# Two column groups in the last stage of a long convolution, identity products at the start, and a new order of work

## The chip, the core and the metric

The kernel runs on one core of one Trainium2 chip. The time is the device time of the slowest core in microseconds (us), here of the only one. TensorE (PE in the profile; PEld is its weight load), VectorE (DVE), ScalarE (ACT), GpSimd (POOL) and SyncE (SP) each work through a queue of their own, in order; 16 DMA engines move data for the transfers that SP and POOL issue.

## The reference, cut to what matters

Two independent heads share the kernel, each of 2048 positions and 1024 channels; their outputs stand side by side.

```python
def _A_ref(q, k, v, shift_k, ssm_k, ssm_D):
    ...
    for t in range(ks):
        k_shift = k_shift + k_pad[:, t:t + S, :] * shift_k[:, ks - 1 - t][None, None, :]
    kv = k_shift * v
    ...
    y_f = kv_f * kf_f[None, :, :, :]
    ...
    y = y + kv * ssm_D[None, None, :]
    return q * y

def _B_ref(x, Lambda_re, Lambda_im, B_re, B_im, C_re, C_im, log_dt, Dskip):
    ...
    for t in range(L):
        h = Lam_bar[None, :] * h + Bu[:, t, :]
    ...
    y = 2.0 * jnp.einsum("blp,dp->bld", hseq, Cmat).real + x * Dskip[None, None, :]
    return y
```

In A, kv_f and kf_f are Fourier transforms along the sequence, padded to 4096; y is the inverse transform of their product. In B, h is a complex state of 1024 entries, and Lam_bar and Bu come from the parameters.

## The kernel before, in words

All work is cut into words such as `U.9.3.0` or `a3.6.0`. The string ORDER (line 67) lists 1504 words; the loop at the end of full_kernel calls the function of each word's name with its numbers (E["a3"](6, 0)). The words' order in the string is thus, engine by engine, the order of each queue: TensorE's, VectorE's, ScalarE's, and also SP's and POOL's, which issue the DMAs. Behind a colon stand the buffers that a word takes: `p3` is PSUM bank 3 (of 8; 128 partitions by 512 columns of 32 bits), `a28` is unit 28 of an arena in SBUF (53 units of 128 by 1024 bf16), `h` and `w` are slots for B's state chunks and for transform weights. A word waits where its data or its buffer is not free. No word is moved at run time.

**Head A** is a transform in stages. kp and vp load k and v; kvm, kva, kvb, kvc (VectorE) make kv for one of 16 residues n2 of the position. Its first three need the shift weights on all partitions: ld_w loads them into one row, wb (TensorE, products with a row of ones, 512 columns) spreads them, wbe (ScalarE) copies them out. Stage 1: am (TensorE, four products of 512 columns in two words for each n2), ae (ScalarE evicts a bank), ast (POOL stores to the DRAM tile Ys_kv). The filter goes the same way, with hl, hT, hc, hm, he, hst, into Ys_h. Stage 2 works on 32 groups, two to a load, 16 loads: lh and lk (SP) read Ys_h and Ys_kv, sh and sk (TensorE, line 650) are transforms of 64 by 64 in the four quadrants of the array, eight products of 512 columns each; she and ske evict; sw (POOL) swaps rows by DMA; pr (VectorE, line 677) multiplies; sa (TensorE, line 689, eight quadrant products) and sae go back; vst (POOL) stores to Vs. No lk can start before all ast have landed, and no vl before all vst.

The last stage: vl (SP, line 705) loads 512 KB of Vs for one of 16 n2; a3 (line 717) makes 512 output columns for all 128 positions of this residue, by two products that add up in one bank. Each takes a weight Gt[:, p, :] of 128 columns, of which those of the other parity are zero. a3e (line 724, ScalarE) evicts; qm or qh (VectorE) multiplies with q, which qp loaded; osp or oh (SP, lines 734 and 732) stores.

**Head B** works in 16 chunks of 128 positions. bl loads the matrix B in 16 parts, bT transposes a part on TensorE by eight products with the identity (line 397), bc copies it out; cl, cT, cc and cx do so for C. Parameters come by ld_par (four small DMAs on SP), par_T (one product, line 255), p32 (VectorE, line 260) and small words; tabA1, tabA2 and sm_pre are tables on VectorE. x (SP) loads a chunk transposed; xs and xl put some chunks aside in DRAM. U (line 444) multiplies it with B: a word is half of a bank, 16 products of 128 columns; ue evicts. r1, r2, sc, r3, r4 (VectorE) rotate, scan along time and rotate back; cy carries the last state over. y (line 527 and, for the skip term, 530) multiplies with C: a word is four products of 512 columns and one of 128, eight words a chunk. For chunks 6 to 12 the word is yt (lines 498 and 512) instead: 16 quadrant products, and 16 small ones in the last part. ye evicts, yst, ysp or yh store 512 or 256 KB.

Of the kernel before, what the change touches and what calls it, by code (L numbers as in the profile page):

```python
# [71 lines left out]
bc.3.0 bl.1.1:a44 bT.1.1:p3 sin1 kva.2 kvb.2:a34 bl.7.1:a46 bT.7.1:p4 bc.3.1 bl.4.0:a45 bT.4.0:p6 bl.7.0:a1 U.0.1.1 bc.1.1 U.0.0.1 bc.7.1 bT.7.0:p7
bc.4.1 bc.4.0 kvb.1:a1 sin2 x.5:a32 U.5.0.0:a50p3 U.5.0.1 U.5.1.0:p4 U.5.1.1 U.5.3.0:p6 bc.7.0 U.5.3.1 U.0.3.1 bl.5.1:a33 bT.5.1:p1 eo ue.5.1 vp.1:a48
bc.5.1 kp.-2 kvm.0:a44 kvc.2 ue.0.3 cl.0.1:a10 kvc.3 cl.1.1:a11 cT.1.1:p7 x.1:a0 U.1.0.0:a48p4 bl.5.0:a9 cx.5.1 kva.0 ue.5.0 bT.5.0:p1 bc.5.0 U.1.0.1
ue.1.0 cT.0.1:p2 cc.0.1 ue.5.3 U.1.2.0:p1 U.1.2.1 cc.1.1 U.1.3.0:p4 U.5.2.0:p6 U.0.2.0:p2 U.0.2.1 stt z2 U.5.2.1 z1 ue.0.1 x.2:a37 ue.0.0 kp.2
kvm.5:a28 kvm.4:a8 vp.0:a38 kvc.1 U.2.0.0:a42p3 U.2.2.0:p7 kvb.0:a36 U.2.3.0:p5 U.2.3.1 U.1.1.0:p0 cl.1.0:a40 kva.4 ue.0.2 r1.0:a4 ue.1.2 ue.5.2 kva.5
gz U.1.1.1 r2.0:h0 dd U.2.1.0:p2 ue.2.3 cx.4.0 am.1.0:p6p5 kvb.5:a41 cx.6.1 rt U.1.3.1 cl.0.0:a33 cT.0.0:p1 sc.0.1 U.2.1.1 ae.1.1.0:a2 ue.1.1 cc.0.0
cl.3.0:a16 cT.3.0:p5 ue.1.3 U.2.2.1 sc.0.0 r1.1:a28 ue.2.1 am.3.1:p4p1 cx.7.0 cc.3.0 ae.1.0.0 r3.0:a16 r2.1:h1 am.1.1:p2p0 ae.1.1.1 r4.0 U.2.0.1
ue.2.0 kvc.0 cT.1.0:p5 cl.2.0:a44 cT.2.0:p6 cc.1.0 x.3:a45 U.3.0.0:a46p0 U.3.2.0:p3 cc.2.0 cl.2.1:a5 cT.2.1:p5 U.3.0.1 cc.2.1 cl.3.1:a4 cT.3.1:p6
ae.3.0.1:a48 ue.2.2 U.3.2.1 ae.1.0.1 am.2.0:p4p5 cc.3.1 U.3.1.0:p2 cx.6.0 U.3.3.0:p7 y.0.0.0:p6 y.0.0.1 r1.2:a16 U.3.3.1 cx.7.1 cy.1 ae.2.0.0:a6  # L80
sc.1.1 sc.1.0 ae.2.1.0 am.2.1:p4p5 ue.3.3 ae.2.0.1 ue.3.0 y.0.0.2 y.0.0.3 kvb.4:a44 am.0.0:p4p7 r3.1:a28 ue.3.2 ae.0.0.0:a4 ae.0.1.0 U.3.1.1 cx.5.0
cx.4.1 y.0.1.0:p0 ue.3.1 vp.2:a38 y.0.1.1 y.0.1.2 kp.3 ae.2.1.1 y.0.1.3 am.3.0:p3p4 kvc.5 am.0.1:p7p2 r4.1 ae.0.0.1 ae.3.1.0 y.1.0.0:p5 ae.0.1.1
ae.3.1.1 kvc.4 y.1.1.0:p7 am.4.0:p4p2 y.1.0.1 y.1.1.1 r2.2:h2 y.1.1.2 hl.1:a42 y.1.1.3 r1.3:a8 ye.0.0:a40 y.1.0.2 cy.2 ae.3.0.0 sc.2.1 am.4.1:p1p3
# [715 lines left out]
```

## Time and profile before

| | us |
|---|---|
| median of 3 runs | 347.86 |
| runs | 347.36 to 350.82 |
| profiled execution, whole | 351.36 |
| its span, first to last instruction | 349.6 |
| TensorE busy in the span | 334.9 |
| VectorE busy in the span | 314.1 |

A line of the profile names the engine, the line of the kernel, the operation, what it writes and reads, and how often; behind a bar stand the group's busy time in us and the mean length of one in ns, then the idle time of the engine before it and what ended that. One product's length holds its way through the pipeline; how fast products follow each other is read from the chain of waits or the timeline, where neighbours are merged into one row (start, length, count). "Granted clock" is the share of TensorE's full clock that the record shows.

### The profile page before, as it was taken

What the parts mean: (1) busy time and instruction counts of PE and PEld (TensorE: products, weight loads), DVE (VectorE), ACT (ScalarE), POOL (GpSimd) and SP (SyncE); (2) the same over time, 40 slices, a digit from 0 to 9 for tenths busy, and PEclk for the clock granted to TensorE, in tenths of its full rate; (3) what the DMA queues carried; (4) which work ended last, traced back from release to release, by engine and by line L of the source; (5) the groups of instructions that cost most, each with busy time, mean ns of one, the idle gap of its engine ahead of it and who ended that gap; (6) DMA issues with size and microseconds to landing.
All of it is one profiled execution on the core that took longest, in us unless ns stands there. A gap on an engine that the chain in (4) does not pass through costs nothing. (4 is left out here: it accounts for less than half of the span.)

```text
span 349.6 us, 10684 instructions
## 1 busy us (share of the span) xinstructions
PE 334.9 (96%) x4540; PEld 236.7 (68%) x4561; DVE 314.1 (90%) x240; ACT 285.2 (82%) x547; POOL 79.4 (23%) x130
## 2 busy tenths in 40 slices
PE   5899999999999999999987999999999999999996
PEld 3799998546765767748863565786668676865442
DVE  4899999999999999999996997979985968997992
ACT  6999997468698999987884889999998887537672
POOL 5000000032334337055231004223233151300100
PEclk9999999999999999999998999999999999999999
DMA  6999967599999999999869599989989999779977
GB/s 204 336 297 257 239 157 79 225 263 281 289 317 295 370 273 316 314 259 303 301 229 367 181 335 310 364 304 347 384 322 321 368 400 344 281 264 389 344 299 266
DMA packets 63691, 103.07 MB, mean 295 GB/s; under 512 B 29550, under 2 KB 31870, under 8 KB 63644
## 3 DMA queue, kind: packets, MB, share of 16 engines
q1 hardware_dynamic: 52348, 63.98, 61.6%
q0 software_dynamic: 11296, 38.42, 30.0%
q8 instruction: 35, 0.57, 0.7%
q14 instruction: 12, 0.10, 0.1%
HBM read 53.09 MB, written 34.60 MB: 251 GB/s over the span
## 5 line engine op out<-in xcount | busy, mean ns | idle before, releaser
L444 PEld LDWEIGHTS <-BT 128*128 128x128 bf16 x2048 | 117.5, 98 | 11.3 <-issue 4.5
L444 PE MATMUL bank<-arena,BT 128*128 128x128 bf16 x2048 | 123.2, 219 | 1.2 <-ACT arena L446 0.5
L472 DVE TENSOR_TENSOR_SCAN gslot<-rtab,gslot 128x1040 bf16<-128x1040 f32 x32 | 73.0, 2310 | 3.0 <-ACT gslot L468 2.8
L527 PE MATMUL bank<-CT,gslot 128*128 128x512 bf16 x279 | 68.4, 379 | 0.7 <-DVE gslot L478 0.2
L498 PE MATMUL bank<-CT,gslot 64*64 64x512 bf16 x896 | 57.4, 384 | 0.0
L446 ACT CAST arena<-bank 128x512 bf16<-128x512 f32 x64 | 40.0, 659 | 13.3 <-PE bank L444 13.2
L677 DVE TENSOR_TENSOR arena<-arena 128x4096 bf16<-128x4096 bf16 x16 | 36.2, 2285 | 10.8 <-ACT arena L667 7.7
L527 PEld LDWEIGHTS <-gslot 128*128 128x128 bf16 x288 | 26.0, 98 | 27.8 <-DVE gslot L478 0.9
L667 ACT CAST arena<-bank 128x512 bf16<-128x512 f32 x64 | 38.5, 685 | 6.6 <-PE bank L650 6.6
L498 PEld LDWEIGHTS <-gslot 64*64 64x64 bf16 x896 | 29.8, 109 | 19.2 <-issue 1.7
L589 ACT CAST arena<-bank 128x512 bf16<-128x512 f32 x64 | 35.7, 632 | 7.8 <-PE bank L583 6.0
L459 DVE TENSOR_TENSOR arena<-arena,Z 128x4096 bf16<-128x4096 bf16 x16 | 36.5, 2282 | 4.7 <-ACT arena L446 4.2
L660 ACT CAST arena<-bank 128x512 bf16<-128x512 f32 x64 | 37.7, 731 | 3.5 <-PE bank L650 3.4
L627 ACT CAST arena<-bank 128x512 bf16<-128x512 f32 x64 | 36.2, 632 | 4.8 <-PE bank L621 4.7
L697 ACT CAST arena<-bank 128x512 bf16<-128x512 f32 x64 | 38.7, 738 | 0.9 <-PE bank L689 0.9
L459 DVE TENSOR_TENSOR arena<-gslot,Z 128x4096 bf16<-128x4096 bf16 x16 | 36.6, 2289 | 1.0
L671 POOL DMA_DIRECT2D arena<-arena x32 | 17.4, 546 | 79.5 <-ACT arena L660 75.3
L563 DVE TENSOR_TENSOR arena<-arena 128x4096 bf16<-128x4096 bf16 (+3 forms) x16 | 30.0, 1885 | 1.2 <-DMA arena<-in_A_k_dram 0.7
L592 POOL DMA_DIRECT2D Ys_kv<-arena x16 | 11.4, 719 | 86.2 <-ACT arena L589 86.2
L630 POOL DMA_DIRECT2D Ys_h<-arena x32 | 23.2, 737 | 24.9 <-ACT arena L627 24.9
L650 PE MATMUL bank<-arena,wslot 64*64 64x512 bf16 x256 | 24.3, 388 | 3.6 <-DMA arena<-Ys_kv 3.2
L536 ACT CAST arena<-bank 128x512 bf16<-128x512 f32 x32 | 20.1, 651 | 8.4 <-PE bank L530 4.7
(101 smaller groups left out, 414.6 us busy)
## 6 DMA issues: line engine op xcount, KB each, us to landing
Ys_kv<-arena POOLq DMA_DIRECT2D x16, 512.0 KB, 5.6
Ys_h<-arena POOLq DMA_DIRECT2D x32, 256.0 KB, 4.7
arena<-Ys_h SPq DMA_DIRECT2D x16, 512.0 KB, 5.5
arena<-arena POOLq DMA_DIRECT2D x32, 256.0 KB, 4.8
...
```

Of the source, the lines that this page charges most:

```text
L444: nc.tensor.matmul(pu[:, w, jl, :], BT[:, 2 * jp + jl, w, d, :], xT[:, d, :], start=(d == 0), stop=(d == ND - 1))
L446: E["ue"] = lambda i, jp: nc.scalar.copy(st["u", i][:, :, 2 * jp:2 * jp + 2, :], st.pop(("pu", i, jp)))
L459: nc.vector.tensor_mul(m, s_, win(Z))
L472: nc.vector.tensor_tensor_scan(gf, rtab[:].rearrange("p j t -> p (j t)"), gf, 0.0, ALU.mult, ALU.add)
L498: mm = nc.tensor.matmul(st["py", i, dh][64 * c:64 * c + 64, :], h[rows, w, j, 2 + 64 * c:66 + 64 * c], CT[rows, j, w, dh * 512:(dh + 1) * ...
L527: nc.tensor.matmul(py, h[:, w, j, 2:GW], CT[:, j, w, dh * 512:(dh + 1) * 512], start=(j == 0 and w == 0), stop=False)
L589: return nc.scalar.copy(st["ysb", n2][:, p, dh * 512:(dh + 1) * 512], st.pop(("pa", n2, p, dh)))
L627: return nc.scalar.copy(st["yh", hf, s][:, p, e, :], st.pop(("pb", hf, s, e, p)))
L660: return nc.scalar.copy(st["hab", i][:, 0, a, l, :], st.pop(("ps", "h", g, l)))
L667: return nc.scalar.copy(st["x16", i][:, a, l, :], st.pop(("ps", "k", g, l)))
L677: nc.vector.tensor_mul(hab, st.pop(("x16", i)).rearrange("p a l d -> p (a l d)").unsqueeze(1).to_broadcast([P, 2, 2 * D]), hab)
L697: return nc.scalar.copy(st["vsb", i][:, a, dh * 512:(dh + 1) * 512], st.pop(("pv", g, dh)))
```

## The change

Four things are done together.

1. G holds for each parity p only the 64 weight columns of its own positions. a3 writes the product with parity p to partitions 64 p to 64 p + 63 of the bank, as a product of its own: 128 rows and 64 columns of the array, without adding up. The 128 partitions then hold the even positions, then the odd ones.
2. qp, oh, osp (and ost, which no word uses) move these rows by two DMAs, one for each parity, of half the bytes each: 17 DMAs more in all.
3. A word wu.n is new: n products of the identity with itself, 128 columns, into a bank that the next word overwrites. Eight of them hold 66 products, all ahead of the first U.
4. ORDER is written anew, 1512 words; words other than wu are the same (beside the tasks that yf names, behind which a yt word is fenced). The tile praw lies in a weight slot.

In the new order ld_par stands behind bl.0.0 and par_T behind five wb words; x.0 stands behind nine bl and three kp words (before: nine and two). The last kv product of VectorE is kvc.12, behind sc.6.0 (before: kvc.14, ahead of sc.6). From the last am word to the first sk, TensorE's words are six U, six sh and six yt (before: seven U, six sh, four yt). yst.7, yst.9, yst.10 and yst.11 stand behind the last vst (before: yst.9; yst.12 and yst.13 do in both), qp.0 among the a3 words (before: all qp ahead of the first vl). Behind the last sa stand 6 yt, 12 U, 24 y and 32 a3 words (before: 2, 10, 24, 32); the a3 words stand in four runs with y and U words between.

```diff
@@ a_constants
-    G = np.stack([tr.T * (m % 2 == p)[None, :] * 2 / NFFT for p in range(2)], axis=1)
+    G = np.stack([tr.T[:, m % 2 == p] * 2 / NFFT for p in range(2)], axis=1)
@@ full_kernel
-    Gt = const.tile([P, 2, P], BF16, name="Gt")
+    Gt = const.tile([P, 2, P // 2], BF16, name="Gt")
...
-        praw = const.tile([4 * NJ, P], BF16, name="praw")
+        praw = wslots[1][0:4 * NJ, 0:P]
...
+    def wu(n):
+        pt = bank()
+        for _ in range(n):
+            nc.tensor.matmul(pt[:, 0:P], ident[:], ident[:], start=True, stop=True)
+    E["wu"] = wu
...
-        spd(st["qt", r], qr[:, 2 * r:2 * r + 2, :])
+        for p in range(2):
+            spd(st["qt", r][64 * p:64 * p + 64, :, :], qr[p::2, 2 * r:2 * r + 2, :])
...
-            nc.tensor.matmul(pt, Gt[:, p, :], st["vv", n2][:, p, dh * 512:(dh + 1) * 512], start=(p == 0), stop=(p == 1))
+            nc.tensor.matmul(pt[64 * p:64 * p + 64, :], Gt[:, p, :], st["vv", n2][:, p, dh * 512:(dh + 1) * 512], start=True, stop=True)
...
-    E["oh"] = lambda n2: spd(oar[:, n2, :], st["ot", n2 // 2][:, n2 % 2, :])
-    E["ost"] = lambda r: gpd(oar[:, 2 * r:2 * r + 2, :], st["ot", r])
-    E["osp"] = lambda r: spd(oar[:, 2 * r:2 * r + 2, :], st["ot", r])
+
+    def halves(dma, rows, tile):
+        for p in range(2):
+            dma(rows[p::2], tile[64 * p:64 * p + 64])
+    E["oh"] = lambda n2: halves(spd, oar[:, n2, :], st["ot", n2 // 2][:, n2 % 2, :])
+    E["ost"] = lambda r: halves(gpd, oar[:, 2 * r:2 * r + 2, :], st["ot", r])
+    E["osp"] = lambda r: halves(spd, oar[:, 2 * r:2 * r + 2, :], st["ot", r])
@@ ORDER
-ld_w:a8 ld_par wb.0:p1 wbc:a12 wb.4:p5 par_T:p2 p32 ld_F wbe.0 wb.7:p3 wb.2:p4 wbe.4 exp1 dve2 dve3 wbe.2 wbe.7 tabA1:a16a18a4a6 sm_pre wb.3:p0
-wb.5:p7 wbe.5 exp2 wbe.3 bl.6.0:a52 bT.6.0:p2 wb.6:p6 kring:a20 bc.6.0 bl.1.0:a1 bl.0.0:a0 bT.0.0:p1 bc.0.0 bl.0.1:a3 bT.0.1:p5 bc.0.1 wbe.6 bl.2.1:a2
-bl.3.0:a52 bT.3.0:p7 kva.3 x.0:a35 kp.-1 kvm.2:a40 kvm.1:a28 bT.2.0:p1 U.0.0.0:a2p0 U.0.3.0:p2 bc.2.0 U.0.1.0:p5 kvb.3:a52 bl.4.1:a0 kva.1 bT.4.1:p1
...
-U.9.0.1 ae.13.0.1 U.7.2.0:p6 ae.13.1.1 U.7.2.1 x.15:a10 hst.1.2.0 am.12.0:p3p2 ae.13.0.0 ae.15.0.0 kva.14 U.7.1.1 r1.6:a12 kvb.14:a0 r2.6:h0 kvc.14
-hst.1.2.1 ue.7.1 hst.1.3.1 am.12.1:p7p0 U.9.1.0:p5 U.9.1.1 ae.14.1.1 ae.14.0.0 ae.14.1.0 U.9.2.1 ue.7.3 ae.12.1.1 hst.1.4.1 hst.1.3.0 sc.6.0 yst.4
-r3.6:a24 ae.12.0.1 hst.1.7.0 ue.9.2 hst.1.4.0 hst.1.5.1 hst.1.5.0 ast.13 lh.1:a28 sh.2:p0p1 sh.3:p3p4 she.2.1:a12 she.2.0 she.3.0 she.3.1 lh.0:a18
-she.1.1 sh.7:p5p3 U.10.0.0:a4p0 U.10.0.1 r2.7:h1 cy.7 she.6.1:a20 ast.15 ast.14 she.7.1 she.7.0 ast.12 sw.1.0 she.6.0 ue.9.3 lk.1:a44 sk.3:p2p7
...
-sw.12.0 sw.14.1 pr.14 sa.28:p5p3 sae.28.1:a48 sae.28.0 sa.29:p6p1 sae.29.1 sae.29.0 sw.12.1 yf.yt.12.ue.13.2 yt.12.1.0 pr.12 sw.13.0 sa.25:p4p7
-sw.13.1 yst.6 pr.13 sa.27:p3p5 yst.7 yt.12.1.1 yst.11 sa.26:p6p1 sae.25.1:a6 sae.27.1:a18 sa.24:p7p5 yt.12.1.2 yt.12.1.3 sae.27.0 U.15.0.0:a44p3
-U.15.0.1 sae.26.1 U.15.2.0:p1 sae.26.0 U.15.2.1 U.14.1.0:p6 r1.13:a32 U.14.1.1 r2.13:h2 cy.13 sae.25.0 U.15.1.0:p4 U.15.1.1 sae.24.1 sae.24.0 sc.13.1
...
-r1.14:a32 r2.14:h0 cy.14 sc.14.1 ye.12.0:a46 ue.15.1 ue.15.2 sc.14.0 ye.12.1 qp.7:a8 r3.14:a24 qp.2:a30 vst.14 vst.13 vst.12 r4.14 yst.9 vl.6:a18
-a3.6.0:p3 a3.6.1:p4 a3e.6.0:a20 a3e.6.1 vl.10:a10 a3.10.0:p2 a3e.10.0:a18 ye.13.0:a17 vl.12:a4 a3.12.1:p1 a3.10.1:p6 a3.12.0:p3 a3e.12.1:a10 vl.14:a14
...
-osp.0 osp.6 a3e.7.0 qm.3 y.15.0.2 osp.3 a3e.11.1 a3e.11.0 qm.5 a3e.9.1 y.15.0.3 qm.4 ye.15.0:a52 osp.4 osp.5 yh.15.0 y.15.1.1 a3e.15.0 y.15.1.2
-a3e.15.1 y.15.1.3 qh.15 ye.15.1 oh.15 yh.15.1
+ld_w:a8 wbc:a12 wu.18:p4 wb.2:p4 wu.2:p3 wb.4:p3 wbe.2 bl.0.0:a52 wu.2:p0 wb.7:p0 wbe.7 wu.2:p7 wb.3:p7 wu.2:p6 wb.0:p6 wbe.4 ld_F ld_par par_T:p1 p32
+exp1 bT.0.0:p4 wbe.3 dve2 dve3 tabA1:a18a16a4a6 sm_pre bl.6.0:a1 bT.6.0:p3 bc.6.0 bl.6.1:a3 bl.0.1:a2 bl.4.0:a0 wu.2:p5 wb.5:p5 bT.0.1:p1 bc.0.1 tabA2
+bT.6.1:p0 bc.6.1 wb.1:p7 bl.1.1:a28 wb.6:p3 bT.1.1:p2 kring:a20 wbe.1 bl.1.0:a29 wbe.5 kp.0 kp.1 wbe.6 bl.2.1:a52 bc.1.1 wbe.0 exp2 kvm.3:a36
+bT.1.0:p1 bl.4.1:a1 bc.0.0 bc.1.0 kp.-1 kvm.1:a44 kva.3 wu.31:p0 bT.4.1:p0 kvm.2:a40 kva.1 bT.2.1:p2 kvb.3:a1 kva.2 sin0 bc.2.1 bT.4.0:p1 par_rest
+x.0:a31 kvb.2:a30 sin1 kvb.1:a52 gz wu.7:p7 U.0.0.0:a28p7 U.0.3.0:p3 bl.2.0:a3 bT.2.0:p5 bc.2.0 U.0.0.1 bl.7.1:a2 bT.7.1:p4 sin2 bl.3.1:a32 bT.3.1:p2
...
+U.7.1.0:p1 ue.7.0 sc.6.0 am.15.1:p3p6 U.7.1.1 ae.13.1.0:a42 ae.13.0.0 am.15.0:p4p0 ae.13.1.1 lw.3:w1 ae.15.1.1:a8 kvc.12 ae.13.0.1 ae.15.0.1 hst.1.1.0
+U.7.3.0:p2 U.7.3.1 yst.4 sc.6.1 U.7.2.0:p6 ae.15.0.0 am.14.1:p7p3 U.7.2.1 ae.15.1.0 r3.6:a12 hst.1.7.1 am.14.0:p4p0 ue.7.3 hst.1.1.1 ue.7.1 x.10:a11
+ae.14.1.1:a46 hst.1.2.1 ue.7.2 U.9.0.0:a32p3 lw.2:w3 U.9.3.0:p1 am.12.1:p2p6 ae.14.0.0 ae.14.1.0 am.12.0:p4p0 ae.14.0.1 ae.12.0.1:a34 U.9.1.0:p7
+ae.12.0.0 x.15:a10 U.9.2.0:p2 ae.12.1.0 U.9.1.1 lw.0:w2 U.9.2.1 ae.12.1.1 U.9.0.1 hst.1.2.0 hst.1.3.0 hst.1.3.1 hst.1.4.0 hst.1.5.1 hst.1.7.0 ye.5.1
+hst.1.4.1 ue.9.1 hst.1.5.0 ue.9.2 ast.13 ast.15 lh.1:a2 sh.3:p6p4 sh.2:p5p7 she.2.0:a24 she.3.1 ue.9.0 r4.6 yt.6.0.0:p0p2 yt.6.0.1 yt.6.0.2 she.3.0
+she.2.1 r1.7:a20 r2.7:h1 lh.0:a30 sh.0:p3p4 cy.7 sh.1:p5p7 lh.3:a28 yt.6.0.3 she.1.0:a4 sh.7:p5p6 she.1.1 ast.14 ast.12 she.0.1 U.9.3.1 she.0.0
+she.7.0:a12 sh.6:p7p3 she.6.1 yf.yt.6.she.7.0 yt.6.1.0 yt.6.1.1 xs.15 lk.1:a2 she.7.1 she.6.0 sk.2:p6p3 ske.2.1:a8 lk.0:a46 sk.3:p7p4 ske.3.0 yt.6.1.2
...
+yt.12.0.1 sw.13.0 sw.13.1 pr.13 sae.24.1:a30 sa.27:p3p1 sae.24.0 sae.25.1 sa.26:p7p6 sae.25.0 yt.12.0.2 yt.12.0.3 U.15.0.0:a8p0 U.15.0.1 U.15.3.0:p2
+U.15.3.1 sae.27.1:a36 r1.13:a20 U.14.3.0:p1 U.14.3.1 sae.26.1 sae.26.0 r2.13:h2 sae.27.0 qp.5:a34 U.14.1.0:p6 U.14.1.1 qp.2:a40 cy.13 ue.15.0 sc.13.0
+ue.14.3 sc.13.1 r3.13:a20 r4.13 ue.14.1 yf.yt.12.ue.15.0 yt.12.1.0 yt.12.1.1 yt.12.1.2 yt.12.1.3 qp.7:a42 y.13.0.0:p7 U.15.1.0:p6 U.15.1.1 ye.12.0:a52
+y.13.0.1 y.13.0.2 y.13.0.3 r1.14:a12 vst.15 r2.14:h0 vst.11 cy.14 vst.14 sc.14.0 vst.12 sc.14.1 vst.13 yst.7 yst.9 yst.10 r3.14:a20 yst.11 vl.2:a2
+vl.11:a36 ue.15.1 ye.12.1 a3.2.0:p3 ue.15.3 a3.2.1:p1 ye.13.0:a0 vl.4:a50 a3e.2.0:a10 a3e.2.1 vl.6:a44 a3.6.0:p6 a3.11.1:p0 vl.5:a46 a3.4.1:p7
+a3e.4.1:a32 a3.4.0:p5 a3.11.0:p4 a3e.11.0:a2 vl.3:a24 a3.3.1:p2 a3.3.0:p1 a3.5.1:p3 a3.5.0:p7 a3e.5.1 U.15.2.0:p4 r4.14 a3e.6.0:a50 a3e.5.0 U.15.2.1
...
+a3e.13.0 qm.6 a3e.8.0 a3.9.0:p7 osp.3 a3.15.0:p0 a3e.9.0 a3e.15.0 y.15.1.0:p1 a3e.8.1 qm.4 y.15.0.0:p3 oh.14 y.15.0.1 y.15.1.1 y.15.0.2 y.15.0.3
+a3e.10.1 y.15.1.2 ysp.14 osp.1 osp.0 osp.6 osp.4 a3e.10.0 qm.5 osp.5 qh.15 ye.15.0:a52 yh.15.0 oh.15 y.15.1.3 ye.15.1 yh.15.1
```

More of the change, by code (lines that the diff above doesn't have):

```diff
@@ L72 @@
[L72 to L83, printed above, removed]
```

146 lines of the change are left out of this document (76 added, 70 removed).

## The prediction

> **What bounds it now.** I read the page's busy table first, then the engines stretch by stretch, then TensorE's waits, and last the timeline and the chain of work around the places where TensorE loses time.
>
> ```profile
> PE 334.9 (96%) x4540; PEld 236.7 (68%) x4561; DVE 314.1 (90%) x240; ACT 285.2 (82%) x547; POOL 79.4 (23%) x130
> ```
>
> ```profile
> 346.20 0.07 PE bank L530
> ```
>
> ```profile
> 80.00:120.00 40.00, 39.74 (x399) 27.29 (x402) 39.97 (x31) 33.79 (x63) 11.82 (x19) 1.00 1.02 302
> 160.00:200.00 40.00, 36.73 (x621) 25.89 (x624) 36.28 (x21) 30.15 (x63) 8.42 (x14) 0.96 0.77 272
> 240.00:280.00 40.00, 39.55 (x736) 28.21 (x732) 33.47 (x18) 37.42 (x79) 11.47 (x19) 1.00 0.99 346
> 310.00:320.00 10.00, 9.95 (x52) 4.79 (x52) 9.72 (x6) 4.10 (x10) 0.00 (x0) 1.00 1.01 362
> ```
>
> The columns of the third fence, behind the stretch, are length, PE, PEld, DVE, ACT, POOL, granted clock, DMA share, GB/s. TensorE is the first bound everywhere: it is idle 349.6 - 334.9 = 14.7 us of the span. But it has partners. In 80 to 120 us VectorE is as full as TensorE (39.97 of 40), in 240 to 280 and in 310 to 320 the DMA engines are (0.99 and 1.01). So microseconds taken from TensorE count in full only if these follow. Its idle time lies at the start, at the end (the chain's last product ends at 346.27, the span at 349.6) and in one place between, where stage 2 waits for the spectra that stage 1 wrote to DRAM:
>
> ```profile
> PE bank L386 <- DMA arena<-in_A_shift_k_dram: 3.6, 1, 3.6
> PE bank L650 <- DMA arena<-Ys_kv: 3.2, 2, 2.1
> ```
>
> ```profile
> 180.67 1.96 PE L444 MATMUL bank<-arena,BT 128*128 128x128 bf16 x32
> 184.73 0.63 PE L650 MATMUL bank<-arena,wslot 64*64 64x512 bf16 x8 [2.10 <-DMA arena<-Ys_kv]
> 185.18 3.38 PE L498 MATMUL bank<-CT,gslot 64*64 64x512 bf16 x32
> 189.03 1.90 PE L498 MATMUL bank<-CT,gslot 64*64 64x512 bf16 x32
> ```
>
> ```profile
> 185.00:190.00 5.00, 5.00 (x68) 2.41 (x64) 3.22 (x3) 3.02 (x7) 0.00 (x0) 0.66 1.03 377
> ```
>
> After the 2.10 us of idleness the granted clock is 0.66 for the next 5 us: 32 products of yt take 3.38 us where the next 32 take 1.90. The place costs 2.1 + 1.1 us of waiting and some 1.5 us of slow clock.
>
> **a3 in column groups.** Before, each a3 word issues two products of 512 columns over the whole array into one bank, half of each weight being zeros.
>
> ```profile
> L717 PE MATMUL bank<-arena,Gt 128*128 128x512 bf16 x62 | 14.5, 379 | 0.1
> L717 PEld LDWEIGHTS <-Gt 128*128 128x128 bf16 x64 | 6.0, 98 | 6.9
> L689 PEld LDWEIGHTS <-wslot 64*64 64x64 bf16 x256 | 7.4, 106 | 6.1 <-DVE arena L677 1.4 <-issue 0.8
> ```
>
> ```profile
> 256.14 0.86 PE bank L498 x16
> 274.53 0.22 PE bank L650 x4
> 274.74 1.91 PE bank L444 x32
> 296.76 0.86 PE bank L689 x16
> 301.20 7.25 PE bank L444 x128
> 334.59 4.32 PE bank L717 x20
> ```
>
> In the chain, 20 products of L717 take 4.32 us, 0.216 each, so the 64 take 13.8. The price of two side by side is read from the quadrant lines: 16 products of 512 columns take 0.86 us at L498 and at L689, four at a time at 0.216 a round. Side by side is thus full speed, also where, as in sk and sh, the two column groups of one row group stream different data (4 in 0.22). That all 128 rows stand under a column group is not in the trace; the bounds are 0 saved and 6.9 saved, and I take 6.9, because the nearest rows show the whole gain for column groups. The new a3 changes the array's shape eight times in the last stage (four runs of a3 among full products), where before there was none; the 64 by 64 words change it 28 times instead of 34. Price: the 32 products at 274.74 behind a quadrant run take 1.91 against 7.25 / 4 = 1.81, so 0.1. Net +0.2 us. Sum of this part: **-6.7 us**.
>
> [...]
>
> **The start.** 66 products of the identity are added.
>
> ```profile
> 1.18 0.28 POOL masks.py:199 TENSOR_SCALAR_AFFINE_SELECT ident<-ident 128x128 bf16<-128x128 bf16 x1
> 2.21 1.30 SPq L402 DMA_DIRECT2D arena<-in_B_B_re_dram  x3
> 3.56 1.01 PE L386 MATMUL bank<-arena,ones 1*128 1x512 bf16 x2 [3.56 <-DMA arena<-in_A_shift_k_dram]
> 4.44 1.86 PE L386 MATMUL bank<-arena,ones 1*128 1x512 bf16 x4
> 4.64 0.19 DVE L260 CAST p<-bank 128x32 f32<-128x32 bf16 x1 [3.65 <-PE bank L255]
> 7.74 1.89 PE L397 MATMUL bank<-ident,arena 128*128 128x128 bf16 x16
> 12.85 2.29 DVE L563 TENSOR_TENSOR arena<-arena 128x4096 bf16<-128x4096 bf16 x1 [0.70 <-DMA arena<-in_A_k_dram]
> 15.71 2.84 PE L444 MATMUL bank<-arena,BT 128*128 128x128 bf16 x48
> ```
>
> Early products are slow: 1.86 / 4 = 0.46 us for 512 columns against 0.216 later, and 16 of 128 columns take 1.89, 0.118 each against 0.057. The first 18 identity products (2.1 us) just fit between the identity's end (1.46) and the first weights (3.56): no cost. The next eight stand between the wb words: 0.9 us. They and the new places of ld_par and par_T (behind five wb, 5 x 0.46) put par_T at 3.56 + 2.3 + 0.9 = 6.8 instead of 4.4 (its eviction starts at 4.64), so VectorE's first work comes 2.4 us later; 0.70 of it was a wait for k anyway, so its first kvm comes +1.7, at some 14.5. wu.31 and wu.7 (38 products, 2.2 us at full clock, 4.5 at the slow one) stand before U.0.0.0, which waits for x.0; x.0's issue moves behind one more k load (1.5 MB instead of 1.0 MB ahead of it, 1.5 us at the 302 to 362 GB/s quoted) but SP, with ld_par behind one load of B, issues that load at about 0.7 instead of 2.21. TensorE, warm sooner, would be ready for U at 13 to 14; I put U.0.0.0 at 15 to 16 against 15.71: **0**, bounds -2 and +4.5.
>
> **The stage boundary.** The order before the last kv product counts: VectorE is full there, so its word list is a clock.
>
> ```profile
> L472 DVE TENSOR_TENSOR_SCAN gslot<-rtab,gslot 128x1040 bf16<-128x1040 f32 x32 | 73.0, 2310 | 3.0 <-ACT gslot L468 2.8
> ```
>
> ```profile
> 164.37 0.68 DVE L578 TENSOR_TENSOR arena<-arena 128x1024 bf16<-128x1024 bf16 x1
> 169.60 1.60 ACT L589 CAST arena<-bank 128x512 bf16<-128x512 f32 x3
> 172.96 0.69 POOL L592 DMA_DIRECT2D Ys_kv<-arena  x1 [0.78 <-ACT arena L589]
> 179.51 1.43 SPq L639 DMA_DIRECT2D arena<-Ys_kv  x3
> ```
>
> Before, kvc.14 comes last, at 164.37; after it kvc.12 does, with one more scan (sc.6.0, 2.31) ahead. With 1.7 of late start it is at 168.4 and ends at 169.1. Then am.12 (four products of 0.216) and four evictions (0.53 each, 2.1) bring POOL to its issue at 172.1, against 172.96 before, where other products stood between kvc.14 and am.12.1. From there as before: 6.55 us to lk's issue, 5.2 to the first sk, so 183.9. TensorE, from am.12 on, has am (0.9), six half U (5.4 by 7.25 / 8), six sh (2.7, by 8 products in 0.45 at 184.73) and six yt (5.2): ready at 169.1 + 14.2 = 183.3. The wait shrinks from 2.1 to about 0.6 us and the clock may then hold. Earlier by 0.8 and up to 2.6 (1.1 + 1.5) saved behind it; I take **-1.5**, bounds -3.5 and +2.
>
> **Stage 2.** Nothing in its products changes, and 5.4 us of TensorE's work leaves it: by words, what follows the last sa is 2 yt, 10 half U, 24 y parts and 32 a3 before (1.7 + 9.1 + 22.3 + 13.8 = 46.9), and 6, 12, 24 and 32 after (5.2 + 10.9 + 22.3 + 6.9 + 0.6 = 45.9; a y part is 0.86 + 0.07). So 6.9 less in all is 1.0 less behind the last sa and some 5.7 before it. The DMA engines were at 0.99 there; the new order moves three B stores of 512 KB out, 1.6 MB, 4.5 us at 346 GB/s, and adds none. qp's second issue costs SP about 0.4 us each, in front of lh and lk. DMA then falls by 4.5 where TensorE falls by 5.7: **+0.7**, bounds 0 and +4.
>
> **The last stage.**
>
> ```profile
> 298.48 0.86 PE bank L689 x16
> ```
>
> ```profile
> 301.94 0.72 POOL L700 DMA_DIRECT2D Vs<-arena  x1 [0.85 <-ACT arena L697]
> ```
>
> ```profile
> 305.95 19.25 SPq L705 DMA_DIRECT2D arena<-Vs  x14
> ```
>
> ```profile
> 306.00:308.00 2.00, 2.00 (x39) 2.00 (x37) 1.97 (x2) 0.59 (x1) 0.00 (x0) 1.00 0.24 30
> 318.00:320.00 2.00, 1.95 (x10) 0.93 (x10) 1.97 (x2) 1.95 (x5) 0.00 (x0) 1.00 1.05 395
> ```
>
> From the last sa (ends 299.3) the span lasts 50.3 us; 6.6 of them pass until the first vl. TensorE needs 45.9 + 3.4 of tail = 49.3. After 305.95 the DMA engines move 16 vl, 8 A stores and 4 B stores of 0.524 MB, 14.7 MB; in the new order qp.0 and about half of four more B stores join, 16.3 MB, 41 to 45 us at 395 to 362 GB/s, so 48 to 52 us with the 6.6. The stores fill the hole at 306 to 308. DMA is thus level with TensorE: **+1.0**, bounds 0 and +3. The halves of qp, osp and oh are 17 more SP issues of the same bytes; the last before the final store come while two y parts (1.9 us) still run, so the tail stays.
>
> **The sum.** -6.7 + 0 - 1.5 + 0.7 + 1.0 = -6.5 us. The profiled execution took 351.36 us (span 349.6 and 1.8 around it); by it 344.9. It stands 3.5 us above the median of the runs, 347.86, and no view shows where. I take the difference from the median: **341.4 us**, the likeliest case's own range 339 to 344.
>
> **The rivals.**
> 1. The waits vanish altogether: boundary -3.5, nothing lost to DMA. -6.7 - 3.5 = -10.2, up to a slightly late start: 338.0. For it: only 14.7 us are idle and 4.7 sit at the boundary; against: 0.99 of DMA. Chance 0.10.
> 2. DMA keeps the pace: stage 2 loses 4 and the last stage 3, -6.7 - 1.5 + 7 = -1.2: 346.7. For it: shares of 0.99 and 1.01; against: 1.6 MB less in stage 2. Chance 0.17.
> 3. The change doesn't do what it says: no overlap, or loads exposed. With 64 loads of 0.106 exposed, 6.8 us go back: 348.2; with no overlap as well 355. Against: the rows of L689 and L444. Chance 0.06.
> 4. Slower: lk and lh come late group by group, because SP issues in order and qp's and xl's waits for slots stand in front of them. A late group idles TensorE; with the clock's loss a stall as at 184.73 costs 2.1 + 1.5 = 3.6. Over 16 groups 0.6 us each undoes the forecast (+9.6: 351.0), three full stalls (+10.8) make 352.2. For it: one such stall exists; against: TensorE waits for no DMA elsewhere in stage 2, with DMA at 0.99. Chance 0.12. [...] The row at 185 shows the loss after 2.10 us, so I leave the price.
>
> The forecast keeps 0.55. **The range**, 338 to 349.5, leaves out half of rival 1, all of 4 and half of 3, 0.20. About 1%, 3.5 us, is what a measurement of this kernel can tell from no change. Faster by over 1% means below 344.4: the forecast and rival 1, 0.65. Within 1% (344.4 to 351.3): rival 2, half of 3 and the near edge of 4, 0.22. Slower: the rest of 4 and of 3, 0.13.
>
> **What would show it.** a3: L717's busy time near 7 instead of 14.5; 20 of its products in 2.2 us. Start: VectorE's first cast near 6.8, U.0.0.0 at 15 to 16. Boundary: the first L650 product on Ys_kv at 184 with under 1 us of wait and a granted clock of 1.00 after it. Stage 2: last sa near 293, no wait of L650 over 1 us. Last stage: DMA share at 1.0 up to the end. Wrong would be: waits of L717 for vl of several us, a second stretch of clock below 0.9, or L717 still at 14.

## The result and the profile after

The change made the kernel slower by a little: 352.32 us (median of 19 runs, 350.35 to 357.58) against 348.91 (19 runs of the kernel before, 347.36 to 351.79), a ratio of 1.008 [1.0055, 1.0105]. One execution, that of 357.58, shows a lower granted clock (0.983, the others 0.989 to 0.996) and takes longer, and the ratios leave it and its like out. The forecast was 341.4 us, with a range of 338 to 349.5. The profiled execution of the changed kernel took 351.44 us with a span of 349.7, by chance the same as that of before (351.36 and 349.6): the run of before that was profiled is one of its longer ones, that of the changed kernel one of its shorter. So the two traces can be laid over each other, and the question is what ate the microseconds that TensorE was to save; the 3.4 us between the medians are not in this pair.

The lines of the changed kernel stand six or seven further down: U is L450, sk L656, sa L695, a3 L724, y L533 and L536, the A stores L742. First the busy table and the groups by line:

```profile
PE 334.3 (96%) x4608; PEld 240.8 (69%) x4627; DVE 314.2 (90%) x240; ACT 285.4 (82%) x547; POOL 79.3 (23%) x130
L724 PE MATMUL bank<-arena,Gt 128*64 128x512 bf16 x64 | 7.7, 383 | 0.0
L387 PE MATMUL bank<-ident 128*128 128x128 bf16 x66 | 7.4, 282 | 1.5 <-POOL ident masks.py:199 1.5
L724 PEld LDWEIGHTS <-Gt 128*64 128x64 bf16 x64 | 3.8, 109 | 3.5 <-issue 1.1
```

a3 fell from 14.5 to 7.7 us, and the identity products added 7.4: TensorE's sum is unchanged (334.9 before), but what was taken lies at the end and what was added at the start. The timeline of TensorE and SP at the end, after and then before (start, length, engine, line, operation, count):

```profile
332.42 2.13 PE L724 MATMUL bank<-arena,Gt 128*64 128x512 bf16 x18
341.93 0.22 PE L536 MATMUL bank<-Dd,arena 128*128 128x128 bf16 x1
334.89 8.52 SPq L742 DMA_DIRECT2D out_dram<-arena  x10
344.67 1.42 SPq L742 DMA_DIRECT2D out_dram<-arena  x2
346.19 0.54 SPq L545 DMA_DIRECT2D out_dram<-arena  x1
```

```profile
346.04 0.22 PE L530 MATMUL bank<-Dd,arena 128*128 128x128 bf16 x1
335.67 7.54 SPq L734 DMA_DIRECT2D out_dram<-arena  x6
346.91 0.33 SPq L539 DMA_DIRECT2D out_dram<-arena  x1
```

TensorE's last product ends at 342.15 instead of 346.27, 4.1 us sooner. The span ends at the same time, so the tail behind it has grown from 3.3 to 7.5 us. What runs in it is seen in the windows of five microseconds (length, PE, PEld, DVE, ACT, POOL, granted clock, DMA share, GB/s), again after and before. From 340 us on only stores are in flight:

```profile
340.00:345.00 5.00, 2.15 (x13) 0.89 (x10) 0.03 (x1) 1.17 (x2) 0.00 (x0) 0.94 0.86 270
345.00:350.00 5.00, 0.00 (x0) 0.00 (x0) 0.00 (x0) 0.00 (x0) 0.00 (x0) 0.50 0.50 157
```

```profile
340.00:345.00 5.00, 4.95 (x28) 2.43 (x27) 2.30 (x3) 1.49 (x4) 0.00 (x0) 1.00 0.94 350
345.00:350.00 5.00, 1.26 (x8) 0.45 (x6) 0.69 (x1) 0.73 (x2) 0.00 (x0) 0.93 0.50 180
```

The same kind of store moved 350 GB/s before and 270 after, with 0.86 of the DMA engines' time still taken (0.94 before): the engines are a little emptier, but above all they move less in the time that they work (270 / 0.86 = 314 GB/s, before 350 / 0.94 = 372). That is the lead that the experiments follow.

### The profile page after: what moved, and what is told of

Its sections match the earlier page's. It is cut to its first block, busy times and chain, and to the rows that moved or that the text cites. A ratio compares the mean times of both kernels' runs of the same rounds, so it can differ in the third digit from the quotient of the medians.

```text
span 349.7 us, 10821 instructions
## 1 busy us (share of the span) xinstructions
PE 334.3 (96%) x4608; PEld 240.8 (69%) x4627; DVE 314.2 (90%) x240; ACT 285.4 (82%) x547; POOL 79.3 (23%) x130
## 4 chain that ended last, share of the span: by engine, by line
PE 63%; ACT 20%; DMA 9%; issue 4%; DVE 1%; POOL 1%; SPq 0%; ACTq 0%; DVEq 0%; POOLq 0%
PE bank L450 24%; PE bank L533 17%; PE bank L504 5%; ACT arena L666 4%; ACT arena L673 4%; DMA arena<-arena 4%; PE bank L589 4%; PE bank L627 3%; DMA arena<-Ys_kv 3%; ACT BT L419 3%; ACT arena L703 3%; PE bank L403 2%; PE bank L611 2%; DMA Vs<-arena 2%; PE bank L695 2%
## 5 line engine op out<-in xcount | busy, mean ns | idle before, releaser
L450 PEld LDWEIGHTS <-BT 128*128 128x128 bf16 x2048 | 117.2, 98 | 9.2 <-issue 3.9
L450 PE MATMUL bank<-arena,BT 128*128 128x128 bf16 x2048 | 122.1, 219 | 1.0 <-ACT BT L419 0.3
L533 PE MATMUL bank<-CT,gslot 128*128 128x512 bf16 x278 | 68.2, 379 | 0.8 <-DVE arena L465 0.2
L452 ACT CAST arena<-bank 128x512 bf16<-128x512 f32 x64 | 39.3, 651 | 14.3 <-PE bank L450 14.1
L533 PEld LDWEIGHTS <-gslot 128*128 128x128 bf16 x288 | 26.0, 98 | 28.3 <-issue 0.8
L595 ACT CAST arena<-bank 128x512 bf16<-128x512 f32 x64 | 35.6, 634 | 10.0 <-PE bank L589 9.4
L633 ACT CAST arena<-bank 128x512 bf16<-128x512 f32 x64 | 35.5, 662 | 4.4 <-PE bank L627 4.0
L703 ACT CAST arena<-bank 128x512 bf16<-128x512 f32 x64 | 36.5, 669 | 1.8 <-PE bank L695 1.8
L673 ACT CAST arena<-bank 128x512 bf16<-128x512 f32 x64 | 36.9, 717 | 0.7 <-ACT arena L666 0.7
L666 ACT CAST arena<-bank 128x512 bf16<-128x512 f32 x64 | 35.9, 695 | 1.4 <-PE bank L656 1.4
L542 ACT CAST arena<-bank 128x512 bf16<-128x512 f32 x32 | 20.4, 649 | 12.0 <-PE bank L536 6.5
L636 POOL DMA_DIRECT2D Ys_h<-arena x32 | 24.2, 775 | 24.0 <-ACT arena L633 24.0
L656 PE MATMUL bank<-arena,wslot 64*64 64x512 bf16 x256 | 24.3, 382 | 0.5 <-ACT arena L673 0.2
```

The source lines that it names most:

```text
L450: nc.tensor.matmul(pu[:, w, jl, :], BT[:, 2 * jp + jl, w, d, :], xT[:, d, :], start=(d == 0), stop=(d == ND - 1))
L452: E["ue"] = lambda i, jp: nc.scalar.copy(st["u", i][:, :, 2 * jp:2 * jp + 2, :], st.pop(("pu", i, jp)))
L533: nc.tensor.matmul(py, h[:, w, j, 2:GW], CT[:, j, w, dh * 512:(dh + 1) * 512], start=(j == 0 and w == 0), stop=False)
L595: return nc.scalar.copy(st["ysb", n2][:, p, dh * 512:(dh + 1) * 512], st.pop(("pa", n2, p, dh)))
L633: return nc.scalar.copy(st["yh", hf, s][:, p, e, :], st.pop(("pb", hf, s, e, p)))
L666: return nc.scalar.copy(st["hab", i][:, 0, a, l, :], st.pop(("ps", "h", g, l)))
```

## Experiments

**Theory A (width):** the cut of each q load and A store into two of 64 neighbouring partitions makes these transfers themselves slower. **Theory B (order):** the new order costs what the column groups save. **Theory C (identity products):** they delay the start, and nothing comes back. All ratios are to the kernel before on the same chip; the experiments ran on several chips.

**One part alone.** The new order was taken off (e1, and the identity products with it), the identity products alone (e3), the halves (e7, with full products and whole transfers); and the halves alone were put into the kernel before (e2).

```diff
# e2_halves, against the kernel before; a3 stays two full products
+    by = np.argsort(m % 2, kind="stable")
+    G = np.stack([(tr.T * (m % 2 == p)[None, :] * 2 / NFFT)[:, by] for p in range(2)], axis=1)
...
+            spd(st["qt", r][64 * p:64 * p + 64, :, :], qr[p::2, 2 * r:2 * r + 2, :])
...
+            dma(rows[p::2], tile[64 * p:64 * p + 64])
```

e1_cols_old_order: 

> The changed kernel with the order of before: column groups and half-partition transfers, no identity products. Theory A (the stores of 64 partitions are slow, 0.74 us of SP each against 0.38 for a whole one of 128, and set the end): TensorE ends about 6 us earlier than the kernel before does, the tail behind it grows from 3.3 to 7 us, so 2 to 4 us faster than before, 345 to 347. Theory B (the new order loses it, the column groups are right): 6 to 7 us faster, 342 to 343. Theory C (the identity products at the start lose it): as B, since none are here. If the DMA engines alone bound the last stage, 1 us faster at most.

e3_no_ident: 

> The changed kernel without its 66 identity products, the rest as it is. Theory C: the first U starts near 16 instead of 19.2, and 2 to 4 us of the total come back (348 to 350). Theories A and B: the stage boundary takes up an earlier start as a wait, so within 1 us of the changed kernel.

e2_halves: 

> The kernel before, in its own order and with its full products, but the columns of G sorted by parity, so that q and A's output move in transfers of 64 partitions as in the changed kernel. Theory A (transfers of 64 partitions move less per time): the tail behind TensorE's last product grows from 3.3 to some 7 us, 3 to 5 us slower than before, 352 to 354. Theory B (the stores are harmless, the new order or a shorter TensorE brings the loss): within 1 us of before.

e7_order_only: 

> The new order with its identity products, but a3 in full products and whole transfers as before. Theory A: TensorE has 6.7 us more to do than in the changed kernel and ends at 347 to 349 of the span, the tail is 3.3 again, so 1 to 3 us slower than before, about as the changed kernel. Theory B (the order is worse, column groups and stores right): 5 us and more slower than before. If the order by itself is better: faster than before by 1 to 2 us.

| | ratio [95%] |
|---|---|
| e1: column groups and halves, old order | 1.0181 [1.0112, 1.025] |
| e2: halves alone | 1.0168 [1.0118, 1.0217] |
| e3: all but the identity products | 1.0081 [1.0039, 1.0123] |
| e7: new order and identity products alone | 1.0048 [1.0018, 1.0078] |

The halves alone cost 1.7%, 5.9 us, more than the whole change does: A holds. The order and the identity products together cost 0.5%; B is a small part. Without the identity products the time is that of the changed kernel (1.0081 against 1.008), so C falls. Its trace shows why they cost nothing that could be seen. TensorE's timeline of e3, then of the changed kernel:

```profile
17.49 3.09 PE L450 MATMUL bank<-arena,BT 128*128 128x128 bf16 x32
20.42 0.61 PE L403 MATMUL bank<-ident,arena 128*128 128x128 bf16 x8
```

```profile
13.17 1.89 PE L403 MATMUL bank<-ident,arena 128*128 128x128 bf16 x16
14.85 2.79 PE L387 MATMUL bank<-ident 128*128 128x128 bf16 x31
17.47 1.50 PE L403 MATMUL bank<-ident,arena 128*128 128x128 bf16 x24
19.20 1.95 PE L450 MATMUL bank<-arena,BT 128*128 128x128 bf16 x32
20.99 0.61 PE L403 MATMUL bank<-ident,arena 128*128 128x128 bf16 x8
```

Without them U comes 1.7 us sooner, but its 32 products take 3.09 us instead of 1.95: the slow products are U's own. At the next transposes the two stand 0.57 us apart.

e1 was expected to be faster than the kernel before by all three theories, and was not: with halves and the old order the column groups save nothing (1.0181 beside e2's 1.0168). Two runs with whole transfers show what they are worth without halves. They leave one of a3's two products out, so that half of each sum is missing, and TensorE loses about as much as by column groups (busy for 334.6 us in e9, 334.3 in the changed kernel, 338.9 in e7): e9 in the new order, e15 in the old.

```diff
-            nc.tensor.matmul(pt, Gt[:, p, :], st["vv", n2][:, p, dh * 512:(dh + 1) * 512], start=(p == 0), stop=(p == 1))
+        nc.tensor.matmul(pt, Gt[:, dh, :], st["vv", n2][:, dh, dh * 512:(dh + 1) * 512], start=True, stop=True)
```

e9_half_work: 

> The new order with its identity products and whole transfers, and of each a3 word only one of the two products is issued, so half of the last stage's sums is left out: TensorE's time of the column groups without the transfers of 64 partitions. Theory A: 4 us faster than the changed kernel, 348 to 349, level with before, the tail back at 3 to 4 us. Theory B: within 1 us of the changed kernel. If TensorE's time counted in full: 342.

e15_half_work_old_order: 

> The kernel before, in its own order, with one of the two products of each a3 word left out: TensorE has 6.9 us less, nothing else differs. If the old order lets TensorE's time count: 3 to 5 us faster than before, as in the new order with half of the products. If in the old order the loads of Vs and VectorE's chain to the last y set the last stage: within 1.5 us of before.

e9 took 346.29 us, 0.9887 [0.9856, 0.9918]; e15 348.86, 0.9964 [0.9937, 0.9991]. From e7 to e9 the saving is 1.6%, 5.6 us of the 6.9 that TensorE loses (32 products of 0.216); from e9 to the changed kernel the halves take back 1.9%, 6.7 us, near e2's 5.9. So the measured 0.8% splits into 0.5 - 1.6 + 1.9. In the old order the same saving gives only 0.4%. In part that is because a3 there comes up against its loads, of which e9 shows no wait (waits of e15, in us, times, longest; in e1 they are 3.9 us in six times):

```profile
PE bank L716 <- DMA arena<-Vs: 2.1, 2, 1.1
```

**Which transfers.** e17 is the changed kernel with the stores of before, e14 with the q loads of before; in both the rows that meet or are stored are then not the right ones, and the bytes are the same. e12 is the same kernel as e17, and e16 the changed kernel once more beside them, on the chip of e17 and e14.

e12_whole_stores: 

> The changed kernel with A's stores as whole transfers of 128 partitions, so that its rows are stored in the order even, odd and not put in place; q still comes by halves. If the stores by halves are what costs: 346 to 348, near the 346.3 of the new order with half of the products. If the q loads by halves cost: 351 to 353, like the changed kernel. If both: between, near 349.

e17_whole_stores: 

> The changed kernel with whole stores (rows not put in place) and q by halves, once more. If the stores by halves cost about half: 3 us faster than the changed kernel, 349 to 350. If nearly all: 346 to 347. If nearly none: 351 to 353.

e14_whole_q: 

> The changed kernel with q loaded by whole transfers of 128 partitions, so that q's rows stand in their old order and meet the wrong rows of A; the stores still go by halves. If the q loads by halves cost about half of the 6 us: 3 us faster than the changed kernel. If nearly all is in the stores: within 1 us of it. If nearly all is in the loads: 5 to 6 us faster, near 346.5.

e16_changed_again: 

> The changed kernel itself, on the chip of the three runs above, so that they are compared with it directly: 351 to 353.5.

e17 took 349.3 us, 0.9971 [0.9935, 1.0008]; e14 350.6, 1.0029 [1.0004, 1.0055]; e12 has no ratio; its two shortest runs took 349.02 and 350.13. Against the changed kernel's 1.008, whole stores are worth 1.1% (3.8 us) and whole q loads 0.5% (1.8 us): both kinds of transfer carry a share, and together they come near e2's 5.9. e16 took 356.08, 1.0137 [1.0054, 1.022], more than the 351 to 353.5 that were expected. Its trace shows one reason: the wait for Ys_kv at the boundary of stage 2 is back, of which the other traces of the new order show 0.2 us at most, and the third pair of sk products comes at 195.21 instead of 190.29:

```profile
191.23 1.06 PE L656 MATMUL bank<-arena,wslot 64*64 64x512 bf16 x8 [2.58 <-DMA arena<-Ys_kv]
```

The stores' share is the tail: in e17 the last product ends at 342.72 and the span at 346.7, 4.0 us later; in e14, with halved stores, 341.90 and 350.1, 8.2 us later. TensorE's last row and the stores' rate (GB/s, last column) in e17, then in e14:

```profile
342.50 0.22 PE L536 MATMUL bank<-Dd,arena 128*128 128x128 bf16 x1
340.00:345.00 5.00, 2.72 (x15) 1.19 (x13) 0.60 (x1) 1.17 (x2) 0.00 (x0) 1.00 0.90 338
```

```profile
341.68 0.22 PE L536 MATMUL bank<-Dd,arena 128*128 128x128 bf16 x1
340.00:345.00 5.00, 1.90 (x12) 0.74 (x8) 0.00 (x0) 1.17 (x2) 0.00 (x0) 1.00 0.84 262
```

**Why halves are slow.** Four reasons are possible: twice the number of DMAs, SP's queue that issues them, the rows in DRAM (every second row), or the partitions (64 neighbours). e13, e10 and e11 cut the q loads and stores of the kernel before in two in other ways; e6 lets POOL issue the second half of each A store of the changed kernel.

```diff
# e10_near_rows: 64 neighbouring partitions, neighbouring rows
+            spd(st["qt", r][64 * p:64 * p + 64, :, :], qr[64 * p:64 * p + 64, 2 * r:2 * r + 2, :])
+            dma(rows[64 * p:64 * p + 64], tile[64 * p:64 * p + 64])
# e11_spread: every second partition, every second row
+            spd(st["qt", r][p:P:2, :, :], qr[p::2, 2 * r:2 * r + 2, :])
+            dma(rows[p::2], tile[p:P:2])
# e13_by_residue: all partitions, one of the two residues
+            spd(st["qt", r][:, e, :], qr[:, 2 * r + e, :])
+            spd(oar[:, 2 * r + e, :], st["ot", r][:, e, :])
# e6_two_queues
+            (dma, gpd)[p](rows[p::2], tile[64 * p:64 * p + 64])
```

e6_two_queues: 

> The changed kernel with the second half of each A store issued by POOL instead of SP. Theory A1 (SP's queue is the limit, at 0.74 us an issue): SP has half of the issues, the tail shrinks from 7.5 to 4 or 5 us, 2 to 3 us faster than the changed kernel. Theory A2 (64 partitions at a time limit the DMA engines): both halves in flight together may still gain, but if the engines handle one after the other, within 1 us. Theory B: within 1 us.

e10_near_rows: 

> The kernel before, its q loads and A stores each cut into two transfers of 64 neighbouring partitions, whose rows in DRAM stand 64 KB apart as in the whole transfer (for the q loads 32 KB). Theory W (64 partitions at a time are slow): 4 to 6 us slower than before, 353 to 356, like the halves by parity. Theory S (rows 128 KB apart in DRAM are slow): within 1.5 us of before. Theory N (twice the number of transfers is slow): 4 to 6 us slower.

e11_spread: 

> The kernel before, its q loads and A stores each cut into two transfers of every second partition, whose rows in DRAM stand 128 KB apart (q 64 KB), as in the changed kernel. Theory W in the form that neighbouring partitions are what is slow: within 1.5 us of before; in the form that any 64 are slow: 4 to 6 us slower. Theory S: 4 to 6 us slower. Theory N: 4 to 6 us slower.

e13_by_residue: 

> The kernel before, its q loads and A stores of pairs cut into two transfers by residue: 128 partitions and 256 KB each, rows in DRAM 64 KB apart (q 32 KB, in pieces of 2 KB instead of 4). Theory N: 4 to 6 us slower than before. Theories W and S: within 2 us of before.

| cut of the transfers | ratio [95%] | q load, store: us to landing | GB/s at 340 to 345 us |
|---|---|---|---|
| before, whole | 1 | 7.0, 3.4 | 350 |
| e13, by residue | 1.0017 [1.0, 1.0035] | 4.2, 2.5 | 352 |
| e11, every second partition | 1.0009 [0.9983, 1.0036] | 4.3, 2.5 | 348 |
| e10, 64 neighbours, near rows | 1.0137 [1.0096, 1.0178] | 5.3, 3.9 | 274 |
| e2, 64 neighbours, every second row | 1.0168 [1.0118, 1.0217] | 5.0, 4.1 | 262 |
| changed kernel, as e2 | 1.008 [1.0055, 1.0105] | 8.4, 3.9 | 270 |

The first row's transfers have 512 KB, the others' 256 (one store in each of the other groups is B's, and in e13, which leaves oh whole, two more are oh's). The landing times stand in the page's table of DMA issues (count, KB each, median us from issue to landing); of e10 and of e11:

```profile
arena<-in_A_q_dram SPq DMA_DIRECT2D x16, 256.0 KB, 5.3
out_dram<-arena SPq DMA_DIRECT2D x15, 256.0 KB, 3.9
```

```profile
arena<-in_A_q_dram SPq DMA_DIRECT2D x16, 256.0 KB, 4.3
out_dram<-arena SPq DMA_DIRECT2D x15, 256.0 KB, 2.5
```

and the rate in the windows of e10, e11 and e2, with only stores in flight:

```profile
340.00:345.00 5.00, 4.36 (x24) 1.99 (x22) 1.15 (x2) 2.11 (x4) 0.00 (x0) 1.00 0.87 274
```

```profile
340.00:345.00 5.00, 4.68 (x26) 2.16 (x25) 1.47 (x2) 1.79 (x4) 0.00 (x0) 1.00 0.94 348
```

```profile
340.00:345.00 5.00, 5.00 (x28) 2.41 (x27) 3.66 (x4) 1.53 (x3) 0.00 (x0) 1.00 0.86 262
345.00:350.00 5.00, 2.71 (x15) 1.19 (x13) 0.69 (x1) 2.15 (x4) 0.00 (x0) 1.00 0.85 261
```

It is not the number of DMAs (e11 has as many as e10, e13 two fewer), and not the rows (near rows are slow, distant ones are not). e2 and e11 use the same rows in as many DMAs, and differ in the partitions (and in the order of G's columns, which doesn't change the work). SP's queue isn't it either. In e11 it issues as densely as in the changed kernel (10 in 8.52 us there), with no loss:

```profile
334.17 9.21 SPq L736 DMA_DIRECT2D out_dram<-arena  x12
```

and e6, which takes half of the A stores off it, ran 1.0065 [1.0039, 1.0092], not clearly better than the change. What is left is which partitions a transfer spans: with 64 neighbours the stores move 262 (e2) and 274 GB/s (e10), with every second partition 348 (e11), with all of them 350 to 352 (before, e13). So with the two halves close behind each other in flight the rate falls by about a quarter. That the partitions are the cause is shown; why 64 neighbours are slower, no run here shows.

**A way round it that fails.** e4 (new order) and e5 (old order) keep the column groups, and each of their q loads and A stores moves 128 partitions, with the rows put in order by the pattern on the DRAM side, [2][64][columns].

```diff
+        spd(st["qt", r].rearrange("p s d -> p (s d)"), qr[:, 2 * r:2 * r + 2, :].rearrange("(m p) s d -> p m (s d)", p=2))
...
+        dma(rows.rearrange("(m p) d -> p m d", p=2), tile)
```

e4_whole: 

> The changed kernel, but no transfer covers 64 partitions: q comes by one transfer of 128 partitions, whose DRAM side runs over even rows, then odd ones; a store of two residues is split by residue, 128 partitions and 256 KB each, a store of one is whole. The number of stores stays 14 for the pairs, so that the width is tested, not the count. Theory A in the form that the 64 partitions are slow: 3 to 4 us faster than the changed kernel, the last store issued within 2 us of TensorE's end. Theory A in the form that the number of issues is what costs: within 1 us. Theories B and C: within 1 us.

e5_cols_whole_old_order: 

> The order of before with the column groups and the 128-partition transfers of the run before this one. Theory A (width): 342 to 344, the whole 6 us. Theory B: 342 to 343 too, but then no better than the run with the order of before and half-partition transfers. If the DMA engines bound the last stage whatever the width: 346 to 348.

By theory A they were to be level with the kernel before or faster; they took 486.7 and 487.25 us, 1.3886 [1.3797, 1.3975] and 1.3897 [1.38, 1.3994]. In e4's SP timeline and a window of its end:

```profile
385.79 28.57 SPq L740 DMA_DIRECT2D out_dram<-arena  x5
```

```profile
440.00:460.00 20.00, 0.00 (x0) 0.00 (x0) 0.00 (x0) 0.00 (x0) 0.00 (x0) 0.50 0.13 51
```

From 400 to 480 us the windows show 51 to 63 GB/s at a DMA share of 0.13 to 0.17; 0.13 of 16 engines is the time of two. The pattern's outermost dimension is 2 here; in the other kernels' q loads and A stores it is 64 or 128. Whether that is what makes these transfers slow, no run tells apart.

No version tried beats the kernel before and keeps the whole sums and their rows; e9, with half of each sum left out, is the fastest of all.

## Why the prediction was wrong, point by point

**a3 in column groups, -6.7: right.** 14.5 us fell to 7.7, and the 18 products at 332.42 take 2.13 us, 0.237 a pair, so 32 pairs take 7.6 instead of 13.8: -6.2. Of what TensorE loses, e7 and e9 show 5.6 us in the whole time. The third rival (loads exposed) fell: two loads of 109 ns and two products of 512 columns fit into 0.237 us, where exposed loads would make it 0.434 (0.216 + 2 x 0.109, an estimate). U's rows of before say the same of full tiles: 128 products, each with a load of 98 ns, take 7.25 us, 57 ns each.

**Start, 0 with bounds of -2 and +4.5: within the bounds.** U came at 19.20 against 15.71, +3.5. The forecast had TensorE warm sooner and U at 15 to 16. That earlier work brings the full rate sooner was an assumption: beside e3 the identity products did so (16.7 us against 19.9), against the kernel before they did not (14.4; estimates, last section). par_T came late too: VectorE's first cast starts at 7.93, forecast for 6.8, before 4.64.

**Boundary, -1.5: near, by another split, and with some luck.** TensorE came later, and so did not wait:

```profile
185.46 0.60 PE L656 MATMUL bank<-arena,wslot 64*64 64x512 bf16 x8
185.90 1.90 PE L504 MATMUL bank<-CT,gslot 64*64 64x512 bf16 x32
190.29 0.63 PE L656 MATMUL bank<-arena,wslot 64*64 64x512 bf16 x8
```

```profile
185.00:190.00 5.00, 5.00 (x105) 3.36 (x98) 4.88 (x4) 4.29 (x10) 1.70 (x4) 1.00 0.88 288
```

The first sk starts at 185.46 (before 184.73) with no wait ahead of it, 32 yt products take 1.90 us instead of 3.38, the clock stays at 1.00, and the third pair of sk stands at 190.29 against 192.14 before. Start and boundary together are -1.85; forecast -1.5. The pair of traces flatters this: at the third pair of sk the profiled run of before is the latest of seven traces in the old order (187.8 to 192.1, median 191.3), while eight in the new order have a median of 190.2 (189.7 to 190.7, and e16 at 195.2). By the medians the new order gains 1.1 us here, less than the old order's traces differ among themselves. Nor is the price of the clock fixed: in e13, after a wait of 2.12 us at the first sk, the clock stays at 1.00 and the next 32 yt products take 1.90 us.

**Stage 2, +0.7 with bounds of 0 and +4: mis-sized, within the bounds.** The last sa ends at 295.2 instead of 299.34, 4.1 us sooner, where the forecast had 293. With 1.85 of that won by the boundary, stage 2 itself gave 2.3 us, where the words that left it are worth 5.7 by the forecast: 3.4 us were given back, not 0.7. (By the forecast's own prices the four yt and two U words that moved are worth 5.3, so 3.0.) Waits for the products of VectorE and the swaps by DMA have grown (windows of after, the same of before, then waits of after):

```profile
200.00:240.00 40.00, 38.29 (x700) 26.72 (x696) 34.33 (x18) 39.57 (x84) 11.30 (x20) 1.00 0.98 330
280.00:300.00 20.00, 18.66 (x358) 13.99 (x347) 16.68 (x10) 15.70 (x32) 7.92 (x13) 1.00 1.03 312
```

```profile
200.00:240.00 40.00, 39.40 (x728) 27.36 (x724) 35.73 (x19) 39.03 (x82) 10.17 (x17) 1.00 0.95 333
280.00:300.00 20.00, 19.77 (x383) 14.24 (x376) 15.56 (x8) 16.34 (x34) 6.10 (x11) 1.00 0.97 357
```

```profile
PE bank L695 <- DVE arena L683: 2.0, 3, 1.3
DVE arena L683 <- DMA arena<-arena: 6.7, 7, 1.5
```

In these 60 us TensorE is busy for 38.29 + 18.66 = 56.95 us, and before for 39.40 + 19.77 = 59.17. The second window holds some 5 us of last-stage work after against 1 before, which waits for nothing, so idle time of TensorE makes about 2.2 of the 3.4 us. DMA share is at 0.98 to 1.03 there, as rival 2 had it.

The halves have a part in this too. Most q loads lie in stage 2, six halves of them here, and while they run the same order moves less by halves (the changed kernel, then its window) than by whole loads (e7's window):

```profile
283.73 4.69 SPq L717 DMA_DIRECT2D arena<-in_A_q_dram  x6
280.00:290.00 10.00, 9.92 (x192) 8.04 (x184) 7.97 (x5) 8.98 (x19) 3.65 (x6) 1.00 1.04 282
```

```profile
280.00:290.00 10.00, 9.92 (x191) 7.99 (x186) 9.88 (x6) 8.98 (x19) 3.64 (x6) 1.00 0.96 346
```

The five traces of the new order with q by halves have 280 to 306 GB/s in this window, the three with whole q loads (e7, e9, e14) 310 to 347. From the third pair of sk to the end of the last sa the five take 104.3 to 106.1 us, the three 102.5 to 104.3: on average 1.9 us less. And e7 and e9 end the last sa at 293.3 and 292.8, where the forecast had it. So more than half of what stage 2 gave back is again the halves; the rest, of the size by which these traces differ among themselves, stays open.

**Last stage, +1.0, and "the halves of qp, osp and oh are 17 more SP issues of the same bytes ... so the tail stays": this is the step that failed.** The same bytes are not the same work. In 64 neighbouring partitions they move at 262 to 274 GB/s instead of 350, and the q loads and A stores are 4.2 MB each, 8.4 in all: 24 us at 350 GB/s, 31 at 270. Not all of these 7 us must show, but e2 showed 5.9 and the step from e9 to the changed kernel 6.7. The forecast gave the halves nothing: its +1.0, with an upper bound of 3, stood for other bytes that move into the last stage. The bound was made of bytes by the rates in windows of whole transfers, the nearest rows that there were, and the shape of a transfer was not taken as an unknown; it should have been, as its rate stood in no row of before. In the traces 4.2 us of the miss are the tail (7.5 against 3.3), forecast to stay. Not all of that is the halves' doing: in e9, with whole transfers, the tail is already 5.5, as TensorE is done sooner (339.34) and the stores are not. Against e9 the changed kernel is 2.5 us later at the last sa, 2.8 at the last product and 4.9 at the end of the span.

The sum by the trace, against the profiled run of before: -1.85 at start and boundary, -4.1 at the last sa, -4.1 at the last product, 0 at the end of the span. The forecast had -6.5 there.

By the ratios, which do not hang on one pair of traces, the change cost 2.8 us, 9.3 more than forecast. Its parts are the order with the identity products, +1.7 (e7) where the forecast had 0 - 1.5 + 0.7 + 1.0 = +0.2; the shorter a3, -5.6 (e7 to e9) instead of -6.7; and the halves, +6.7 (e9 to the changed kernel) instead of nothing. Another 1.1 us of the distance from 341.4 to 352.32 lie in the base: the median of three runs, 347.86, became 348.91 with nineteen.

Rival 2 (DMA keeps the pace, 346.7) was the nearest in kind, with too small a price; rival 4 (loads late in stage 2, 351 to 352) named a time near the measured one by another mechanism, loads of lk and lh that come late. Those did not: all the idle time ahead of sk and sh in the profiled run of the changed kernel is 0.5 us (in e16 lk did come late, once for 2.58 us).

```profile
L656 PE MATMUL bank<-arena,wslot 64*64 64x512 bf16 x256 | 24.3, 382 | 0.5 <-ACT arena L673 0.2
```
